# Load order at the start, and the row layout of w2, in an attention and MLP training step

## The chip, the cores and the metric

The kernel runs on one core of one Trainium2 chip. The metric is device time in microseconds, the median of several executions. Most executions of one kernel lie within 0.3% of each other. Ratios are the mean time of one kernel's runs over the mean of the other's runs of the same rounds, so they are not quite the ratio of the medians quoted beside them.

Engines: PE multiplies matrices (PEld is its weight load), DVE and ACT work element by element, POOL and SP here mostly issue DMA. SBUF is the core's on-chip memory of 128 partitions, PSUM the one that PE writes its sums to. The profile's line numbers (L451) are lines of the kernel; the change shifts them by one to ten.

## The reference

Forward and backward pass of a decode step: one token, 32 heads of attention over a cache of 8,192 positions, plus a gated MLP, in bf16. All gradients are outputs.

```python
xn = layernorm(x)                                  # D = 640
q = xn @ wq                                        # 32 heads of 128
p = softmax(q . k_cache * 128**-0.5)               # per head, 8192 positions
a = (p @ v_cache) @ wo
b = (silu(xn @ w1) * (xn @ w3)) @ w2               # F = 1728
out = x + a + b
# outputs: out and the gradients of x, k_cache, v_cache, wq, wo, w1, w3, w2
```

K, V and their gradients are 2 MB per head each. They make up 268 of the 304.6 MB that are moved. w1, w2 and w3 are 2.2 MB each.

## The kernel before

Ten SBUF slots of 2 MB hold K and V tiles. A head's K tile is overwritten by the gradient of K, stored, and its slot is loaded with a later tile; V likewise. Loads and large stores go through one queue, SP's, in program order. The MLP runs once, between heads 1 and 2, and borrows four slots (`mA` to `mD`). Its gradients go out through POOL's queue.

```python
load_group(0, nc.sync)              # wq and wo of heads 0 to 3: rows of 1,024 and 1,280 B
for _ in range(4):
    load_next()                     # K0, V0, K1, V1: 16,384 B per partition
mC = free_slots.pop(0); mD = free_slots.pop(0); ...
w2a = mD[:, 0:NBA * D].rearrange("p (b c) -> p b c", c=D)          # NBA = 12
fifo(w2a, B_w2[0:NBA * P, :].rearrange("(fb p) c -> p fb c", p=P)) # row fb*128+p: 1,280 B pieces
fifo(w1a, ...); ...                                                # then w1, w3, K2, V2

def store(kind, h):
    t = kv_tiles.pop((kind, h))
    ...
    fifo((dkc if kind == "K" else dvc)[h], t[:])   # gradient out
    free_slots.append(t)
    load_next()                     # next load; it waits until its slot's store has landed

def mlp():
    for wi in range(2):             # gate and up
        for b, rows in blocks_f:    # 13 blocks of 128 hidden units and one of 64
            for ci in range(NC):
                nc.tensor.matmul(gu_ps[0:rows, wi, b:b + 1],
                                 lhsT=wrow(wi, ci)[:, b * P:b * P + rows], rhs=xn_col_bf[:, ci:ci + 1], ...)
    ...                             # w2a * g, summed on PE; hcol, dgu from the sums
    for b in range(NBA):
        nc.vector.tensor_scalar(w2a[:, b, :], g_bc[:], hcol[:, b:b + 1], None, ALU.mult)
    nc.gpsimd.dma_start(out_8[0:NBA * P, :].rearrange("(fb p) c -> p fb c", p=P), w2a)
    ...
    for wi in range(2):
        for b0 in range(0, NB, 4):
            ...                     # PE turns dgu columns into rows, in PSUM tile pb
            nc.scalar.copy(bc_sb[:, wi, f0:f1], pb[:, 0:f1 - f0])
    ...                             # w1 and w3: products with bc_sb, gradients, stores by POOL
```

## Time and profile before

| | before |
|---|---|
| median of the first three runs, us | 749.35 (748.56 to 749.82) |
| profiled run, us | 747.4 |
| bytes moved, mean rate | 304.6 MB, 409 GB/s |
| steady rate, 160 to 300 us | 425 GB/s |

The page of the kernel before, cut: the engines' busy time, the DMA share and the rate in 40 equal slices of the span, and the chain of work that ended last.

```profile
PE 596.1 (80%) x11263; PEld 568.4 (76%) x11263; DVE 447.8 (60%) x739; ACT 333.4 (45%) x668; POOL 30.4 (4%) x45
...
DMA  8999999999999999999999999999999999999991
GB/s 327 387 413 421 426 425 425 395 427 426 416 426 427 428 421 428 425 428 425 424 424 429 426 425 417 415 417 424 420 413 425 418 417 419 419 415 418 408 402 72
...
DMA 48%; PE 39%; DVE 8%; issue 2%; ACT 1%; SPq 0%; ACTq 0%; DVEq 0%
```

No engine is full, but the DMA row reads 9 in 38 of 40 slices. So this kernel is bound by DMA, and the question for any change is whether it makes bytes move faster or keeps the DMA engines from running out of work. The rates name the weak places: the first two slices, the eighth (395), and the last (72).

The view by stretches resolves them. After the stretch and its length stand the busy times of PE, PEld, DVE, ACT and POOL; the last three numbers are granted PE clock, DMA share and GB/s.

```profile
2.00:4.00 2.00, 0.00 (x0) 0.00 (x0) 0.69 (x3) 1.09 (x1) 0.00 (x0) 1.00 0.57 139
4.00:6.00 2.00, 0.00 (x0) 0.00 (x0) 0.00 (x0) 0.00 (x0) 0.00 (x0) 1.00 0.77 201
...
28.00:34.00 6.00, 4.75 (x81) 4.29 (x80) 0.53 (x3) 5.07 (x11) 0.00 (x0) 1.00 1.05 333
...
130.00:135.00 5.00, 4.74 (x82) 4.68 (x83) 2.90 (x2) 3.36 (x7) 0.00 (x0) 1.00 0.97 382
135.00:140.00 5.00, 5.00 (x96) 4.86 (x94) 1.28 (x7) 4.15 (x10) 0.00 (x0) 1.00 1.00 367
```

At 28 to 34 us the share is full but the rate is 333: small packets. By the trace's packet records, w2's 1,280 B packets took a mean of 63.4 ns on each of 16 engines, which is 16 x 1,280 / 63.4 or 323 GB/s; K's and V's 16,384 B packets took 621 ns, 422 GB/s. At 130 to 140 us the packets are large, and yet the rate drops.

The timeline around that dip (start, length, engine, line, what):

```profile
116.55 0.33 SPq L101 DMA_DIRECT2D kv<-in_A_v_cache_dram  x1
116.93 0.81 SPq L101 DMA_DIRECT2D out_dram<-kv  x1
...
120.36 2.28 DVE L379 TENSOR_TENSOR kv<-qd,U 128x4096 bf16<-128x4096 bf16 x1
...
130.25 0.33 SPq L101 DMA_DIRECT2D kv<-in_A_k_cache_dram  x1
130.62 0.59 SPq L101 DMA_DIRECT2D out_dram<-kv  x1
```

DVE finishes the gradient of K of head 2 at 122.64 us, but its store is issued at 130.62. In between, SP holds a load that waits until the w3 gradient's store has left slot `mB`. The ready store stands behind it: SP's queue is in order.

How long the MLP's stores take is in the DMA view (queue, count, KB each, median us from issue to landing; the first line is w1's and w3's gradients, the second w2's):

```profile
out_dram<-kv POOLq DMA_DIRECT2D x2, 1728.0 KB, 37.0
out_dram<-kv POOLq DMA_DIRECT2D x1, 1920.0 KB, 24.2
```

The MLP itself, in the timeline: the gate and up products, the ACT copies of gradient rows, and the first DVE product that needs them.

```profile
55.82 1.21 PE L451 MATMUL gu_ps<-xn_col_bf,kv 128*128 128x1 bf16 x43
59.37 3.24 PE L451 MATMUL gu_ps<-xn_col_bf,kv 128*128 128x1 bf16 x97 [2.34 <-issue]
...
72.29 3.48 ACT L525 CAST kv<-pT 128x512 bf16<-128x512 f32 x8 [3.76 <-PE pT L520]
...
75.24 4.16 DVE L533 TENSOR_TENSOR KT<-kv,kv 128x1024 bf16<-128x1024 bf16 x7
```

### The profile page before, as it was taken

To read this page: it belongs to the slowest core of one execution; us is meant where nothing else is said; L and a number is where in the kernel's file an instruction comes from. 1 tells how busy PE (TensorE), PEld (TensorE's weight loads), DVE (VectorE), ACT (ScalarE), POOL (GpSimd) and SP (SyncE) were. 2 spreads that over 40 slices of the span, in tenths; PEclk is the share of its full clock that TensorE was granted. 3 is DMA by queue.
4 is the path that set the end of the run, shared out by engine and by line. 5 is a ranking of instruction groups with operands and counts; after the bars stand their busy time and mean duration, and the time that the engine had idled before them with its cause. 6 is when DMAs were issued, how large, how long until landed. Compare 5 with 4: busy or idle time off the path is not lost.

```text
span 745.6 us, 25013 instructions
## 1 busy us (share of the span) xinstructions
PE 596.1 (80%) x11263; PEld 568.4 (76%) x11263; DVE 447.8 (60%) x739; ACT 333.4 (45%) x668; POOL 30.4 (4%) x45
## 2 busy tenths in 40 slices
PE   1987698999999779888787897778798788979920
PEld 1886598988998778877686896778798787869820
DVE  4169937677767456656555763646556664656580
ACT  1641055555565355535355553445454353554500
POOL 0100200000000100001000000000000000000000
PEclk9997799999999889999999999998999899988965
DMA  8999999999999999999999999999999999999991
GB/s 327 387 413 421 426 425 425 395 427 426 416 426 427 428 421 428 425 428 425 424 424 429 426 425 417 415 417 424 420 413 425 418 417 419 419 415 418 408 402 72
DMA packets 29136, 304.63 MB, mean 409 GB/s; under 512 B 2836, under 2 KB 5972, under 8 KB 12644
## 3 DMA queue, kind: packets, MB, share of 16 engines
q1 hardware_dynamic: 22736, 276.39, 88.5%
q0 software_dynamic: 5984, 26.30, 8.8%
q8 instruction: 88, 1.44, 0.7%
q10 hardware_dynamic: 308, 0.33, 0.1%
q14 instruction: 20, 0.16, 0.1%
HBM read 151.67 MB, written 151.34 MB: 406 GB/s over the span
## 4 chain that ended last, share of the span: by engine, by line
DMA 48%; PE 39%; DVE 8%; issue 2%; ACT 1%; SPq 0%; ACTq 0%; DVEq 0%
DMA kv<-in_A_k_cache_dram 31%; PE pT L274 17%; DMA out_dram<-kv 13%; PE hb L358 6%; PE hb L373 4%; PE sA L293 4%; DMA kv<-in_A_v_cache_dram 4%; PE dA L293 4%; DVE kv L379 3%; DVE U L365 1%; PE sA L320 1%; PE dh_ps L462 1%; PE hb L363 1%; PE acc L536 1%; PE gu_ps L451 1%
## 5 line engine op out<-in xcount | busy, mean ns | idle before, releaser
L274 PE MATMUL pT<-ident_f,kv 128*128 128x128 f32 x2048 | 337.1, 289 | 67.4 <-DMA kv<-in_A_k_cache_dram 62.4
L276 ACT COPY KT<-pT 128x512 f32<-128x512 f32 x512 | 299.3, 586 | 182.6 <-PE pT L274 149.4
L274 PEld LDWEIGHTS pT<-ident_f,kv 128*128 128x128 f32 x2048 | 224.6, 145 | 71.5 <-issue 69.6
L293 PEld LDWEIGHTS <-KT 128*128 128x128 bf16 x4096 | 196.8, 100 | 17.7 <-issue 10.6
L379 DVE TENSOR_TENSOR kv<-qd,U 128x4096 bf16<-128x4096 bf16 x64 | 146.0, 2284 | 0.0
L379 DVE TENSOR_TENSOR kv<-qd,P 128x4096 bf16<-128x4096 bf16 x64 | 143.4, 2282 | 0.0
L293 PE MATMUL dA<-cz,KT 128*128 128x64 bf16 x2048 | 107.6, 197 | 8.0 <-ACT qd L310 5.8
L293 PE MATMUL sA<-cz,KT 128*128 128x64 bf16 x2048 | 102.7, 192 | 0.4 <-issue 0.3
L358 PEld LDWEIGHTS <-kv 128*128 128x128 bf16 x2048 | 81.7, 106 | 16.5 <-issue 16.5
L358 PE MATMUL hb<-P,kv 128*128 128x64 bf16 x2048 | 82.3, 202 | 14.3 <-DVE U L365 14.3
L375 ACT COPY od_g<-hb 128x2 f32<-128x2 f32 x32 | 5.1, 160 | 160.9 <-PE hb L373 160.9
L373 PE MATMUL hb<-U,kv 128*128 128x64 bf16 x2048 | 70.8, 194 | 5.1 <-issue 5.1
L373 PEld LDWEIGHTS <-kv 128*128 128x128 bf16 x2048 | 66.9, 98 | 6.0 <-issue 5.8
L349 DVE SCALAR_TENSOR_TENSOR U<-dA,P 128x64 bf16<-128x64 f32 x32 | 7.4, 232 | 93.7 <-PE dA L293 93.7
L316 DVE TENSOR_REDUCE mrow<-sA 128x1 f32<-128x64 f32 x32 | 7.2, 224 | 79.5 <-PE sA L293 79.5
L365 DVE SCALAR_TENSOR_TENSOR U<-dA,hb,P 128x128 bf16<-128x128 f32 x32 | 11.4, 355 | 36.3 <-PE hb L363 36.3
L429 DVE SCALAR_TENSOR_TENSOR wq_g<-wq_g,side 128x512 bf16<-128x512 bf16 x40 | 27.3, 683 | 0.0
L340 DVE RECIPROCAL rZ<-sA 128x1 f32<-128x1 f32 x32 | 5.4, 168 | 35.9 <-PE sA L334 35.0
L233 DVE SCALAR_TENSOR_TENSOR side<-wo_g,g_bc 128x640 bf16<-128x640 bf16 x32 | 26.2, 818 | 0.3
L323 DVE TENSOR_REDUCE negM<-sA 128x1 f32<-128x128 f32 x32 | 9.3, 291 | 18.6 <-PE sA L320 18.6
L424 POOL DMA_DIRECT2D out_dram<-wo_g x8 | 6.1, 761 | 295.5 <-DVE cz L298 262.3
L433 POOL DMA_DIRECT2D out_dram<-wq_g x8 | 6.9, 863 | 254.3 <-DVE wq_g L431 254.3
(134 smaller groups left out, 311.5 us busy)
## 6 DMA issues: line engine op xcount, KB each, us to landing
out_dram<-kv SPq DMA_DIRECT2D x64, 2048.0 KB, 31.8
kv<-in_A_k_cache_dram SPq DMA_DIRECT2D x32, 2048.0 KB, 26.9
kv<-in_A_v_cache_dram SPq DMA_DIRECT2D x32, 2048.0 KB, 26.9
out_dram<-wo_g POOLq DMA_DIRECT2D x8, 640.0 KB, 12.1
out_dram<-wq_g POOLq DMA_DIRECT2D x8, 640.0 KB, 13.3
wq_g<-in_A_wq_dram POOLq DMA_DIRECT2D x7, 640.0 KB, 13.8
wo_g<-in_A_wo_dram POOLq DMA_DIRECT2D x7, 640.0 KB, 19.5
kv<-in_B_w_dram SPq DMA_DIRECT2D x2, 1728.0 KB, 16.1
```

What stands on the lines that cost most here:

```text
L233: nc.vector.scalar_tensor_tensor(junk[:], G_["wo"][:, hh, :], 1.0, g_bc[:], ALU.mult, ALU.mult, accum_out=G_["do"][:, hh:hh + 1])
L274: nc.tensor.transpose(pT[:, k * P:(k + 1) * P], W3[:, 4 * c + k, :], ident_f[:])
L276: nc.scalar.copy(KT[:].rearrange("p k w -> p (k w)"), pT[:])
L293: nc.tensor.matmul(S_[kind][:, 0:J], lhsT=KTb[:, k, par, :], rhs=S_["cz"][:, o:o + J], start=(i == 0 and par == 0), stop=(par == 1), skip_ ...
L320: nc.tensor.matmul(S_["K"][:, J:J + P], lhsT=S_["mrow"][:].to_broadcast([P, P]), rhs=ident_f[:], start=False, stop=True, skip_group_check= ...
L323: nc.vector.tensor_reduce(S_["negM"][:], S_["K"][:, J:J + P], AX.X, ALU.max, negate=True)
L358: nc.tensor.matmul(S_["hb"][:, 0:RW], lhsT=V3[:, j, :], rhs=S_["P2"][:, j, 0:1].to_broadcast([P, RW]), start=(j == 0), stop=(j == J - 1), ...
L363: nc.tensor.matmul(S_["hb"][:, 2 * RW:2 * RW + 1], lhsT=negones_b, rhs=S_["rdot"][:], start=False, stop=True, skip_group_check=True)
L365: nc.vector.scalar_tensor_tensor(S_["U2"][:], S_["V"][:, 0:J].unsqueeze(2).to_broadcast([P, J, 2]), S_["hb"][:, 2 * RW:2 * RW + 1], S_["P2 ...
L373: nc.tensor.matmul(S_["hb"][:, RW:2 * RW], lhsT=K3[:, j, :], rhs=S_["U2"][:, j, 0:1].to_broadcast([P, RW]), start=False, stop=(j == J - 1) ...
L379: nc.vector.tensor_tensor(dst[:, lo * DH:hi * DH].rearrange("p (j a b) -> p j a b", a=DH // 2, b=2), vec.rearrange("p (a b) -> p a b", b=2 ...
L429: nc.vector.scalar_tensor_tensor(wq_g[:, ci, :], wq_g[:, ci, :], 1.0, dqb, ALU.mult, ALU.mult, accum_out=dxa[:, ci, g:g + 1])
```

## The change

The intent: start the transfer stream with large packets, and move w2 and its gradient in 15,360 B packets (twelve consecutive rows on each partition) in place of 1,280 B pieces. The second has a price. Hidden unit 12p + b now sits on partition p, block b, so the gate and up products must take w1's and w3's columns twelve apart, and the gradient rows must be scattered back into order.

```diff
+    load_next()
     load_group(0, nc.sync)
-    for _ in range(4):
+    for _ in range(3):
         load_next()
 ...
-    fifo(w2a, B_w2[0:NBA * P, :].rearrange("(fb p) c -> p fb c", p=P))
+    fifo(w2a, B_w2[0:NBA * P, :].rearrange("(p fb) c -> p fb c", fb=NBA))
 ...
+    def fcols(row, b, rows):
+        if b < NBA:
+            return row[:, 0:NBA * P].rearrange("p (f b) -> p b f", b=NBA)[:, b, :]
+        return row[:, b * P:b * P + rows]
 ...
-    ... lhsT=wrow(wi, ci)[:, b * P:b * P + rows],
+    ... lhsT=fcols(wrow(wi, ci), b, rows),
 ...
-        nc.gpsimd.dma_start(out_8[0:NBA * P, :].rearrange("(fb p) c -> p fb c", p=P), w2a)
+        nc.gpsimd.dma_start(out_8[0:NBA * P, :].rearrange("(p fb) c -> p fb c", fb=NBA), w2a)
 ...
+                if b0 < NBA:
+                    nc.scalar.copy(bc_sb[:, wi, 0:NBA * P].rearrange("p (f b) -> p b f", b=NBA)[:, b0:b0 + bn, :],
+                                   pb[:, 0:bn * P].rearrange("p (b f) -> p b f", f=P))
+                    continue
```

More of the change, by code (lines that the diff above doesn't have):

```diff
@@ L450, in mlp @@
                 for ci in range(NC):
-                    nc.tensor.matmul(gu_ps[0:rows, wi, b:b + 1], lhsT=wrow(wi, ci)[:, b * P:b * P + rows],
+                    nc.tensor.matmul(gu_ps[0:rows, wi, b:b + 1], lhsT=fcols(wrow(wi, ci), b, rows),
                                      rhs=xn_col_bf[:, ci:ci + 1], start=(ci == 0), stop=(ci == NC - 1))
```

## The prediction

> **What bounds the kernel now.** DMA. The page's DMA row reads 9 in all slices but the first and last; 304.6 MB move at a mean of 409 GB/s, and in steady stretches (the view by stretches) at 420 to 433 GB/s with a share of 1.0. PE is busy 80%, DVE 60%. In the DMA queue's waits, 544 us are loads waiting for a store to free a slot. So only DMA time counts. Four places lose some:
>
> 1. 2 to 6 us: share 0.57 to 0.77, 139 to 201 GB/s. The weight group goes first, in 1,024 and 1,280 B packets (mean 67 and 62 ns on 16 engines: 245 to 332 GB/s). K of head 0 lands at 15.1 us (chain of waits).
> 2. The w2 load, 28 to 34 us: 1,536 packets of 1,280 B, 282 to 364 GB/s.
> 3. The w2 gradient's store (issued 75.0 us, landed 24.2 us later), in 5,120 B packets: beside 16,384 B packets it got 205 of 840 KB per 2 us.
> 4. 130 to 140 us: 382 and 367 GB/s. K's gradient of head 2 was ready at 122.6 us, but its store was issued at 130.6, behind a load that waited for the w3 gradient's store.
>
> **What changes.**
> - K first: 16 KB packets start the stream, the small ones queue behind. I take most of the 1.3 us idle in 2 to 6 us: -1.0 us. Weights land at about 13.5 us instead of 9; the four DVE products on them (3.5 us) end near 17, when K's transposes are done, so head 0 starts as before or 1 us sooner.
> - w2 in 15,360 B packets: 1.97 MB at 332 GB/s is 5.9 us, at the 422 of the 16 KB packets 4.7: -1.3 us. The store, 404 to 422 GB/s: -0.2 us. The Trainium skill ("DMA: Bandwidth & Descriptors", Queues, rings and completion order) says each DMA engine alternates between queues packet by packet; the 205 to 640 KB in place 3 agrees (5,120/16,384). With near-equal packets the store should land in about 12 us, the other gradients' stores follow sooner, and the dip of place 4 shrinks: -1 us.
> - Strided weights: 120 of the 140 weight loads of the gate and up products read columns 24 B apart. The skill ("SBUF — State Buffer", note on cachelines) says bf16 strides beyond 8 elements pay a penalty; no run here shows it yet. They now run at about 30 ns a pair; at an estimated 55 to 110 ns that is 3 to 9 us, and it delays the MLP, since DVE and PE finish there together (62.6 us). Six ACT copies of 620 ns get a scattered output, maybe twice as slow: up to 1.5 us more.
> - But in 60 to 95 us the queues hold 15 us or more of issued work, so an MLP late by 3 to 6 us starves nothing at once, and head 2's stores now wait 4 to 8 us anyway. I charge +0.5 us.
>
> Sum: -3 us. Predicted 746.0 us, 8 times in 10 between 742.0 and 750.0. Faster by over 2%: 0.01; within: 0.97; slower: 0.02.
>
> **In the profile after:** 2 to 6 us near 400 GB/s; w2's load over 400 GB/s; its store landing in 10 to 16 us; 130 to 140 us over 400 GB/s; gate/up weight loads slower and the MLP several us longer, with DMA share still 1.0.
>
> **What would make it wrong:** an MLP over 8 us late, leaving the queues empty before head 2's stores; small packets costing as much behind K as before; w2's store taking turns from loads that heads 2 to 4 wait for.

## The result, and the profile after

| | before | after |
|---|---|---|
| median of 6 runs, us | 749.0 (747.93 to 749.82) | 746.48 (746.32 to 747.02) |
| ratio | 1 | 0.9969, interval 0.9956 to 0.9982 |
| profiled run, us | 747.4 | 746.44 |

The gain is 0.3%: clear of the noise, and inside the class "same" at 2%. The page after, cut to the rates and the chain:

```profile
GB/s 338 402 414 422 425 428 427 426 424 425 425 424 424 426 421 427 426 429 424 424 421 420 425 419 410 418 416 423 423 410 424 411 424 400 421 416 417 407 402 74
...
DMA 49%; PE 36%; DVE 8%; ACT 2%; issue 1%; SPq 0%; ACTq 0%; DVEq 0%
```

In the first half three slices differ by more than 10: the first two (338 and 402 in place of 327 and 387) and the eighth (426 in place of 395). The same stretches as above:

```profile
2.00:4.00 2.00, 0.00 (x0) 0.00 (x0) 0.69 (x3) 0.95 (x1) 0.00 (x0) 1.00 0.65 218
4.00:6.00 2.00, 0.00 (x0) 0.00 (x0) 0.00 (x0) 0.00 (x0) 0.00 (x0) 1.00 0.93 361
...
28.00:34.00 6.00, 4.75 (x89) 4.30 (x86) 0.77 (x5) 5.09 (x10) 0.00 (x0) 1.00 0.96 371
...
130.00:135.00 5.00, 4.50 (x133) 4.30 (x131) 3.57 (x5) 0.62 (x2) 0.00 (x0) 1.00 1.03 431
135.00:140.00 5.00, 4.61 (x81) 4.55 (x82) 3.62 (x2) 3.23 (x7) 0.00 (x0) 1.00 0.99 423
```

The stores of the MLP's gradients take ten to twelve microseconds less from issue to landing. On the clock they land 4 to 8 us sooner, as all are issued later (w2's at 91.75 us in place of 99.21, w3's at 126.17 in place of 130.23):

```profile
out_dram<-kv POOLq DMA_DIRECT2D x2, 1728.0 KB, 24.9
out_dram<-kv POOLq DMA_DIRECT2D x1, 1920.0 KB, 14.6
```

And the blocked store is gone. In the timeline, SP's load of the freed slot goes at 126.19 us, while DVE is still at work on the gradient of K of head 2, and the store follows DVE's end (128.37) at once. Two things moved here: the load goes 4.1 us sooner, and the gradient is ready 5.7 us later than before, because the MLP is late. So the store itself is issued only 2.2 us sooner; the list under e8 shows why that is enough.

```profile
126.09 2.28 DVE L380 TENSOR_TENSOR kv<-qd,U 128x4096 bf16<-128x4096 bf16 x1
...
126.19 0.33 SPq L101 DMA_DIRECT2D kv<-in_A_k_cache_dram  x1
128.40 0.34 SPq L101 DMA_DIRECT2D out_dram<-kv  x1
```

The MLP, on the other hand, is 6.1 us later:

```profile
55.47 2.68 PE L457 MATMUL gu_ps<-xn_col_bf,kv 128*128 128x1 bf16 x43
58.59 5.68 PE L457 MATMUL gu_ps<-xn_col_bf,kv 128*128 128x1 bf16 x97 [0.45 <-issue]
...
74.38 6.92 ACT L530 CAST kv<-pT 128x512 bf16<-128x512 f32 x3 [3.90 <-PE pT L526]
...
81.33 4.17 DVE L543 TENSOR_TENSOR KT<-kv,kv 128x1024 bf16<-128x1024 bf16 x7 [3.92 <-ACT kv L530]
```

By the chain of waits, the first 43 strided pairs of weight load and product took 2.52 us, 59 ns each, where they had taken 1.05 us, 24 ns each. The three scattered copies took 2.31 us each, where all eight of before, six of them this large, took 3.48 us. DVE waits 3.92 us for them. So the change makes 6 us of engine work in the MLP appear, and still the kernel is faster.

### A ruler for small differences

Differences of 1 us drown in a total of 749. A better ruler is the time at which the first N MB have been moved, taken from the packet records of each trace: bytes summed in order of the packets' starts, instruction packets left out, times from the start of the span and interpolated between packets. The kernel before reaches 10, 20, 52, 60, 150 and 302 MB at 28.02, 53.68, 129.71, 149.88, 362.72 and 727.99 us. This table gives the difference to it, in us (negative is sooner):

| run | 10 MB | 20 MB | 52 MB | 60 MB | 150 MB | 302 MB |
|---|---|---|---|---|---|---|
| before again (e7) | -0.11 | -0.24 | -0.39 | -0.42 | -0.38 | +0.50 |
| the change | -0.56 | -1.14 | -1.69 | -2.83 | -2.71 | -0.94 |
| the change again (e0) | -0.59 | -1.21 | -1.43 | -2.19 | -2.03 | -0.26 |
| e1, K first | -0.58 | -0.54 | -0.68 | +1.33 | +1.52 | +1.12 |
| e2, w2 layout | -0.25 | -1.03 | -1.39 | -2.63 | -2.56 | -1.05 |
| e3, w2 load only | -0.16 | -0.78 | -0.69 | -1.75 | -1.70 | -0.60 |
| e4, w2 store only | -0.06 | -0.09 | -0.37 | -1.53 | -1.53 | -0.40 |
| e5, MLP late | -0.11 | -0.23 | -0.55 | -1.19 | -0.80 | +0.31 |
| e6, copy order | -0.56 | -1.17 | -1.45 | -2.79 | -2.50 | -1.17 |
| e8, K first, store order | -0.52 | -0.49 | -0.77 | -1.95 | -1.72 | -0.52 |

The first 10 MB hold the start, 10 to 20 MB the w2 load, 52 to 60 MB the dip. The two profiles of the same kernel before agree within 0.42 us up to 150 MB and part by 0.9 us after that, so only the columns up to 150 MB are used as a ruler.

### The profile page after: what moved, and what is told of

The parts are those of the page before. It is cut to its first block, busy times and chain, and to the rows that moved or that the text cites. A ratio compares the mean times of both kernels' runs of the same rounds, so it can differ in the third digit from the quotient of the medians.

```text
span 744.7 us, 25012 instructions
## 1 busy us (share of the span) xinstructions
PE 598.0 (80%) x11263; PEld 570.5 (77%) x11263; DVE 448.0 (60%) x739; ACT 344.0 (46%) x668; POOL 29.9 (4%) x45
## 4 chain that ended last, share of the span: by engine, by line
DMA 49%; PE 36%; DVE 8%; ACT 2%; issue 1%; SPq 0%; ACTq 0%; DVEq 0%
DMA out_dram<-kv 25%; PE pT L275 15%; DMA kv<-in_A_k_cache_dram 15%; DMA kv<-in_A_v_cache_dram 8%; PE hb L359 5%; PE sA L294 4%; PE hb L374 4%; DVE kv L380 4%; PE dA L294 3%; DMA wo_g<-in_A_wo_dram 2%; PE gu_ps L457 1%; ACT kv L530 1%; DVE U L366 1%; PE dh_ps L468 1%; PE sA L321 1%
## 5 line engine op out<-in xcount | busy, mean ns | idle before, releaser
L366 DVE SCALAR_TENSOR_TENSOR U<-dA,hb,P 128x128 bf16<-128x128 f32 x32 | 11.4, 355 | 36.2 <-PE hb L364 36.2
L311 ACT CAST qd<-dA 128x256 bf16<-128x256 f32 x31 | 11.5, 373 | 12.4 <-DVE kv L380 9.5
## 6 DMA issues: line engine op xcount, KB each, us to landing
out_dram<-wq_g POOLq DMA_DIRECT2D x8, 640.0 KB, 13.5
```

The source lines that it names most:

```text
L311: nc.scalar.copy(qd[:].rearrange("p a d -> p (a d)"), hd[h].pop("ps_r"))
L366: nc.vector.scalar_tensor_tensor(S_["U2"][:], S_["V"][:, 0:J].unsqueeze(2).to_broadcast([P, J, 2]), S_["hb"][:, 2 * RW:2 * RW + 1], S_["P2 ...
```

## The experiments

All but two gave right results; e3 and e4 are wrong on purpose. "Before" is the median of the before kernel in the same rounds.

| run | before, us | this, us | ratio (interval) |
|---|---|---|---|
| e1 K first | 748.71 | 748.51 | 0.9997 (0.9984 to 1.0009) |
| e2 w2 layout | 748.71 | 746.71 | 0.9976 (0.9963 to 0.9988) |
| e3 w2 load only | 748.71 | 747.09 | 0.9982 (0.9970 to 0.9995) |
| e4 w2 store only | 748.71 | 746.80 | 0.9977 (0.9963 to 0.9990) |
| e5 MLP late | 748.55 | 748.97 | 1.0002 (0.9989 to 1.0014) |
| e6 copy order | 748.55 | 746.26 | 0.9973 (0.9959 to 0.9986) |
| e0 the change again | 748.55 | 747.30 | 0.9978 (0.9966 to 0.9991) |
| e7 before again | 748.82 | 749.05 | 1.0002 (0.9989 to 1.0015) |
| e8 K first, store order | 748.82 | 747.47 | 0.9986 (0.9974 to 0.9999) |
| e10 copy and store order | 748.82 | 746.41 | 0.9968 (0.9954 to 0.9981) |
| e11 w1, w3 rows | 748.43 | 747.32 | 0.9983 (0.9969 to 0.9997) |

My theory after the result: only DMA time counts; the gain is the sum of the start, the w2 load, and a dip that went because a ready store is no longer stuck behind a waiting load; the late MLP costs nothing. The rivals are named in each expectation.

### e1: K first alone

```diff
+    load_next()
     load_group(0, nc.sync)
-    for _ in range(4):
+    for _ in range(3):
```

> Before with K of head 0 first, nothing else. Theory (the start is worth about half a microsecond, read from the two traces: the first 10 MB were moved 0.56 us sooner): 0.3 to 1.0 us less than before; 10 MB moved about 0.5 us sooner; dip at 130 to 140 us still there (about 375 GB/s). Rival (the order at the start is worth 1 us or more, and the whole 2.5 us could come from it): 1.5 us less or better.

The start gains what was expected: 10 MB 0.58 us sooner. The total does not: 0.2 us by the medians, a ratio of 0.9997, short of the 0.3 us that was expected. The stretches and SP's issues show where it went:

```profile
130.00:135.00 5.00, 5.00 (x84) 4.84 (x83) 1.78 (x2) 4.18 (x8) 0.00 (x0) 1.00 0.74 263
135.00:140.00 5.00, 5.00 (x101) 4.95 (x98) 3.13 (x7) 3.90 (x9) 0.00 (x0) 1.00 0.99 321
```

```profile
132.29 0.33 SPq L101 DMA_DIRECT2D kv<-in_A_k_cache_dram  x1
132.67 0.83 SPq L101 DMA_DIRECT2D out_dram<-kv  x1
```

The dip got deeper: 263 and 321 GB/s, a share of 0.74, and head 2's K store is issued at 132.67 us, 2 us later than before. Between 52 and 60 MB this kernel loses 2.0 us. By the ruler more than was won at the start is given back there: at 60 MB this kernel is 1.33 us behind. The total does not show that excess.

### e2: the w2 layout alone

```diff
     (the whole change, except:)
-    load_next()
     load_group(0, nc.sync)
-    for _ in range(3):
+    for _ in range(4):
```

> The change without K first: both w2 transfers in 15,360 B packets, with the strided weight loads and the scattered ACT copies. Theory (load 0.7 us, stores and the dip at 130 to 140 us 1.4 us): 1.5 to 2.2 us less than before, no dip. Rival (layout gives back in the late MLP what it wins in transfers): within 0.5 us of before.

2.0 us less, as the theory had it, and no dip (424 GB/s over 130 to 140 us). Nearly all of the change's gain is in the layout. The rival, that the late MLP gives the layout's gain back, falls.

### e3: only the w2 load (wrong results)

```diff
-    fifo(w2a, B_w2[0:NBA * P, :].rearrange("(fb p) c -> p fb c", p=P))
+    fifo(w2a, B_w2[0:NBA * P, :].rearrange("(p fb) c -> p fb c", fb=NBA))
```

> Before with only the w2 load in 15,360 B packets; no stride anywhere, results wrong on purpose (rows of w2 meet the wrong hidden units). Theory: 12 MB are moved 0.7 to 1.2 us sooner, and the dip at 130 to 140 us stays, as the store still has 5,120 B packets: 0.5 to 1.2 us less in all. Rival (the load alone makes the whole gain): 2 us less.

Partly missed. Between 10 and 20 MB it gains 0.62 us, as expected for the load. But the dip is gone too, though the store still has 5,120 B packets and still takes 24.2 us:

```profile
130.00:135.00 5.00, 5.00 (x91) 4.92 (x88) 2.60 (x2) 3.74 (x8) 0.00 (x0) 1.00 1.02 423
135.00:140.00 5.00, 5.00 (x94) 4.87 (x92) 1.76 (x7) 4.15 (x9) 0.00 (x0) 1.00 1.01 426
```

In this run the load that blocks SP was issued at 127.81 us in place of 130.25. By the packet records, SP's queue moved only 57 GB/s at 116 to 118 us and nothing at 118 to 120 (188 and nothing in the kernel before), so POOL's stores had the engines to themselves for longer and were done sooner. That 2.4 us is enough to close the dip, although the ready store (DVE ends at 122.36) still waits 5.8 us, to 128.19. The dip is thus an edge: a shift of about 2 us of one store, either way, opens it (e1) or closes it (e3). Why the shift went this way with this edit is read from one profile and is an argument, not a test.

### e4: only the w2 gradient's store (wrong results)

```diff
-        nc.gpsimd.dma_start(out_8[0:NBA * P, :].rearrange("(fb p) c -> p fb c", p=P), w2a)
+        nc.gpsimd.dma_start(out_8[0:NBA * P, :].rearrange("(p fb) c -> p fb c", fb=NBA), w2a)
```

> Before with only the w2 gradient's store in 15,360 B packets; no stride, MLP as early as before, results wrong on purpose (rows of the gradient in other places). Theory (larger packets win larger turns, the stores behind them land sooner, so no load holds up head 2's K store): store lands in 10 to 15 us instead of 24, the w1 and w3 stores land 8 to 10 us sooner, no dip at 130 to 140 us, 1.0 to 1.6 us less. Rival (the dip went because the MLP is 6 us late, not because of packets): dip stays near 375 GB/s and the time is within 0.5 us of before.

As the theory said, except that its 1.9 us by the medians lies a little over the range, and that w1's and w3's stores land 7.7 us sooner after their issue (29.3 in place of 37.0), not 8 to 10:

```profile
out_dram<-kv POOLq DMA_DIRECT2D x2, 1728.0 KB, 29.3
out_dram<-kv POOLq DMA_DIRECT2D x1, 1920.0 KB, 14.8
```

```profile
130.00:135.00 5.00, 5.00 (x84) 4.84 (x83) 1.51 (x2) 4.18 (x8) 0.00 (x0) 1.00 1.00 423
135.00:140.00 5.00, 5.00 (x101) 4.96 (x98) 3.13 (x7) 3.90 (x9) 0.00 (x0) 1.00 1.01 428
```

The MLP is as early here as before, so its lateness is not needed for the dip to go. Of the 1.53 us at 60 MB, 1.16 us come between 52 and 60 MB.

The gains of e3 (1.6 us) and e4 (1.9 us) do not add up to that of e2 (2.0 us), because each alone closes the same dip, and it can be closed once.

### e5: the MLP late, all packets as before

```diff
-                nc.scalar.copy(bc_sb[:, wi, f0:f1], pb[:, 0:f1 - f0])
+                for _ in range(5):
+                    nc.scalar.copy(bc_sb[:, wi, f0:f1], pb[:, 0:f1 - f0])
```

> Before with every ACT copy of the MLP's gradient rows made five times over (same values): the MLP ends about 6 us later, all packets as before. Theory (an MLP late by 6 us starves nothing, and does not remove the dip either): within 0.7 us of before, GB/s at 130 to 140 us or some us after still low. Rival 1 (lateness removes the dip): 1 us or more less than before, no dip. Rival 2 (lateness costs time): 1.5 to 6 us more.

The first w1 store is issued at 90.0 us in place of 82.2, the last w3 store at 100.2 in place of 92.3. The time is 748.97 us against 748.55, a ratio of 1.0002. So an MLP 8 us late costs nothing that can be measured. The rates say that lateness also softens the dip:

```profile
130.00:135.00 5.00, 4.20 (x100) 3.85 (x97) 2.39 (x7) 2.09 (x4) 0.00 (x0) 1.00 1.00 393
135.00:140.00 5.00, 4.53 (x106) 4.38 (x103) 5.00 (x3) 1.72 (x4) 0.00 (x0) 1.00 1.01 401
```

393 and 401 in place of 382 and 367, and 0.64 us between 52 and 60 MB: about half of the dip. This did not reach the total, and rival 1, that lateness alone makes the gain, falls. But the store is no longer blocked in this run. Its gradient is ready at 130.21 us, in place of 122.64, and it goes at once, about as late as before:

```profile
129.34 0.33 SPq L101 DMA_DIRECT2D kv<-in_A_k_cache_dram  x1
130.23 0.34 SPq L101 DMA_DIRECT2D out_dram<-kv  x1
```

So lateness removes the block and puts itself in its place. That it is free fits the 8 us that the store had waited for its turn anyway.

### e0: the change again

Unedited, for comparison with e5 and e6 on the same chip.

> The change itself on this chip, for comparison with the runs beside it: 2.0 to 3.0 us less than before, 382 and 367 GB/s of before at 130 to 140 us replaced by over 415.

Missed by some tenths: 1.25 us less by the medians, 1.65 by the ratio. The first set of runs gave 2.5 us by the medians and 2.3 by the ratio (1 - 0.9969, of 749). The intervals overlap; the honest size of the gain is about 2 us. The stretch 130 to 140 us moved at 414 GB/s here, just under the 415 that were expected, and the gain between 52 and 60 MB is 0.76 us in place of 1.14. Head 2's K store is issued at 129.71 us, when its late gradient is ready.

### e6: the same values, copied in another order

```diff
-  nc.scalar.copy(bc_sb[:, wi, 0:NBA * P].rearrange("p (f b) -> p b f", b=NBA)[:, b0:b0 + bn, :],
-                 pb[:, 0:bn * P].rearrange("p (b f) -> p b f", f=P))
+  nc.scalar.copy(bc_sb[:, wi, 0:NBA * P].rearrange("p (f b) -> p f b", b=NBA)[:, :, b0:b0 + bn],
+                 pb[:, 0:bn * P].rearrange("p (b f) -> p f b", f=P))
```

> The change with the six scattered ACT copies walking the output in runs of four neighbouring bf16 (8 B) instead of single ones 24 B apart; same values. If the stride of the write made them slow (2.32 us against 0.60): 0.6 to 1.2 us each, MLP 3 to 5 us shorter. If not: still 2.3 us or more, as the read of PSUM now jumps 512 B. Theory on time (MLP lateness is free): within 0.7 us of the change in either case. Rival (lateness costs): 1 to 2 us less than the change if the copies get faster.

The copies fall from 2.31 to 0.52 us each (three in 1.56; one instruction alone lasts 0.62 us in the median, as expected), and DVE no longer waits for them:

```profile
74.46 1.56 ACT L530 CAST kv<-pT 128x512 bf16<-128x512 f32 x3 [3.70 <-PE pT L526]
...
77.41 4.16 DVE L543 TENSOR_TENSOR KT<-kv,kv 128x1024 bf16<-128x1024 bf16 x7
```

Compared with the change, the w1 products start 3.9 us sooner (77.41 us in place of 81.33). The total is 746.26 us, where the change had 746.48 in its first rounds and 747.30 beside this run; by the ratios 0.9973 and 0.9978, whose intervals overlap widely. Up to 60 MB its ruler agrees with the change's within 0.25 us. So 3.9 us saved on ACT and DVE are worth nothing clear of the noise. The comparison with the change's first rounds (746.48) agrees with the theory; the one beside it differs by 1.04 us in medians, over the 0.7 of the theory and inside the rival's 1 to 2 us, but by the ratio only 0.4 us.

### e9: runs of two bf16

```diff
+  for j in range(0, bn, 2):
-  ... [:, :, b0:b0 + bn], pb[:, 0:bn * P] ...
+  ... [:, :, b0 + j:b0 + j + 2], pb[:, j * P:(j + 2) * P] ...
```

> As the version with the reordered copy, but each copy writes runs of two bf16 (4 B) 24 B apart, 256 elements each, 12 copies. If the cost sits on writes of a single bf16 (4.5 ns each in the change's copies): 0.3 to 0.45 us a copy. If it sits on every separate run: 128 runs of 4.5 ns, 0.7 us a copy or more. Time as the version with the reordered copy.

The group view of that line (least, median and greatest ns of one instruction):

```profile
L531 ACT CAST kv<-pT x12: 391/474/551, 74.9 to 78.0; 128x256 bf16<-128x256 f32 x12
```

The median is 0.47 us, just over the range of the first reading; the timeline has six of them in 1.80 us, 0.30 each. The cost is thus not one per separate run. It sits on single bf16 values written 24 B apart: 4.5 ns per element there, 1.0 with runs of four, 1.2 with runs of two. The one run was 746.55 us, its state unknown.

### e7: before again

> The kernel before, unchanged, for a second profile of it and as a control of the timing. Its ratio should be 1.000 within 0.0013. If the late part of the first profile of before (its run was 747.4 us against a median of 749.0) was a lucky one, this profile moves the same 302 MB 1 us or more later, with the same dip at 130 to 140 us.

749.05 against 748.82 us, ratio 1.0002. The profile has the same dip (409 and 360 GB/s) and moves 302 MB 0.5 us later than the first one, and 0.9 us later when counted from 150 MB. So a part of what looks like a loss of the change after 150 MB in the table belongs to a lucky first profile; the expected 1 us or more was too much.

### e8: K first, and head 2's store ahead of the waiting load

This is the direct test of the blocked store: the kernel with the deepest dip, with one load moved behind one store.

```diff
 def store(kind, h):
     ...
     free_slots.append(t)
-    load_next()
+    if (kind, h) != ("V", 2):
+        load_next()
+    if (kind, h) == ("K", 2):
+        load_next()
```

> K first alone (748.5 us) with one more edit: the load issued behind head 2's V store is moved behind its K store, so that the K store no longer stands behind a load that waits for the w3 gradient's store. All packets of w2 as before. Theory (the dip is that blocked store, which empties the queue): K store of head 2 issued by about 124 us instead of 132.7, 130 to 140 us at over 400 GB/s instead of 292, 1.5 to 2.5 us less than before. Rival (the slow 1.0 to 1.9 us packets of that stretch have another cause, for example the mix of loads and stores): dip stays, time within 0.7 us of before.

SP's issues, and the stretches:

```profile
123.23 0.34 SPq L101 DMA_DIRECT2D out_dram<-kv  x1
129.90 0.34 SPq L101 DMA_DIRECT2D kv<-in_A_k_cache_dram  x1
```

```profile
130.00:135.00 5.00, 4.12 (x71) 4.07 (x72) 3.44 (x2) 2.86 (x6) 0.00 (x0) 1.00 1.02 432
135.00:140.00 5.00, 5.00 (x83) 4.85 (x82) 0.69 (x5) 4.03 (x10) 0.00 (x0) 1.00 1.00 423
```

The store goes at 123.23 us, 9.4 us sooner than in e1, and the dip is closed, from 263 and 321 to 432 and 423 GB/s, with not one packet changed. At 60 MB e8 is 3.3 us ahead of e1. The rival (mixed traffic as such) falls: in the kernel with K first, the blocked store is the cause of the dip.

The other profiles sharpen this. What goes with the dip is how late the store is issued, whether it was blocked or its data were late:

| K store of head 2 issued, us | waited after its data, us | GB/s, 130 to 140 us |
|---|---|---|
| 132.67 (e1) | 11.4 | 292 |
| 130.62 (before), 130.08 (e7) | 8.0, 8.2 | 374, 385 |
| 130.23 (e5) | 0.0 | 397 |
| 129.71 (e0) | 0.0 | 414 |
| 128.40 (the change), 128.19 (e3), 127.90 (e2) | 0.0, 5.8, 0.0 | 427, 424, 424 |
| 126.72 (e6), 124.73 (e10), 123.68 (e4), 123.23 (e8) | 3.6, 0.0, 2.6, 0.0 | 426, 422, 425, 427 |

How a late store lowers the rate is seen only in part. In the kernel before, 14.4 packets are in flight on average at 130 to 132 us, where steady stretches have 16.1: some engines have no work. But at 136 to 138 us the share is 1.05, and 16,384 B packets take 862 ns on average in place of 621. Both are gone in e8 (16.1 in flight, 615 ns). Why the packets slow down is not shown.

In total the time is 747.47 us, 1.35 us less than before by the medians and 1.0 by the ratio; e1 had 0.2. That is right in sign and less than the 1.5 to 2.5 us that were expected. The intervals of e8 and e1 overlap, so the gain of the reorder over e1 is shown by the rates and the ruler, and not by the total.

### e10: copy order and store order on the change

```diff
     (the edit of e6 and the edit of e8, on the change)
```

> The change with the reordered copy and head 2's K store ahead of the load. The change has no dip left, so theory says the store order adds nothing: 745.5 to 746.8 us, no more than 0.7 us from the version with the reordered copy alone (746.3). Rival (there is still time lost behind blocked stores): 1 us or more less.

746.41 us, ratio 0.9968; e6 had 0.9973. As expected: where the dip is gone, the store order has nothing left to win.

### e11: w1 and w3 in consecutive rows as well

The experiments pointed to a layout whose permutation costs no engine time: five consecutive rows of the input dimension per partition for w1, w3 and wq. Then only the five columns of x that are made at the start are permuted.

```diff
-    w1_v = B_w1.rearrange("(ci p) f -> p ci f", p=P)
+    w1_v = B_w1.rearrange("(p ci) f -> p ci f", ci=NC)      # likewise w3, wq and the three gradients
 ...
+    (x and grad_out columns made in the same order; the gradient of x stored from [128, 5], 10 B each)
```

> The version with the reordered copy, and w1, w3, wq and their gradients with five consecutive rows of the input dimension per partition, so that w1 and w3 move in 13,824 B packets instead of 3,456 (loads) and 6,912 (stores). The permutation falls on the five columns of x that are made once at the start, so no strided weight load in the MLP and no scattered copy comes with it. Theory (only DMA time counts): 3.9 MB at 400 GB/s become 421: 20 MB moved 0.4 to 0.6 us sooner than with the reordered copy alone, w1 and w3 stores land sooner, 0.3 to 0.8 us less in all, about 745.7 us; hardly clear of the noise, so the moved bytes decide. Rival (3,456 B is large enough, nothing to win): 20 MB at the same time within 0.15 us.

Missed. Its ratio to before is 0.9983, e6's 0.9973; it beats nothing. Between 12 and 16 MB, where w1 and w3 are loaded, it gains 0.5 us on e6 by the packet records, as intended, but the first 12 MB come 0.27 us later than in e6, and at 20 MB it is 0.15 us behind. At 302 MB the two are equal (0.05 us apart). The end costs more: the last DMA is issued at 727.68 us and the span ends at 745.5, 17.8 us later; in e6 it is issued at 728.36 and the span ends at 744.4, 16.0 us later. The gradient of x goes out there in 128 packets of 10 B in place of 5 of 256 B. They are not what lands last: in both runs that is the gradient store issued at 716.8 to 716.9 us, which lands at 744.37 in e11 and 743.28 in e6. The 10 B packets run until 738.5 us. That they hold the last store up is possible, but no run separates it. No version here beats the change clear of the noise.

## Why the prediction was right

The prediction was 746.0 us in a range of 742.0 to 750.0; measured were 746.48. It was right in total and in its mechanism. The range was wide enough to hold the kernel before itself (749.0), so that lying inside it says little; the terms say more. One by one:

- **"K first: ... -1.0 us."** The mechanism held, the size was twice too large. The engines' idle time at 2 to 6 us did not all go: 218 and 361 GB/s, not "near 400", and 8 to 10 us runs at 303. Small packets did not cost as much behind K as before: those of 1,024 B took 52 ns in place of 67. (The 62 ns of the prediction mixes wo's packets, 56 ns, with w2's, 63.4.) 10 MB are moved 0.5 us sooner (e1: 0.58, before again: 0.11). Alone it is worth nothing in total, because the dip deepens (e1). The landing of the weights was put at 13.5 us; the first DVE product that needs wo starts at 14.38, and the four end at 17.9 in place of 17. Head 0's PE work ends 0.36 us sooner (38.37 in place of 38.73 us).
- **"w2 in 15,360 B packets: ... -1.3 us."** About half: 0.6 us between 10 and 20 MB (the change 0.58, e3 0.62, e2 0.78, before again 0.13). The term took 422 GB/s for w2's new packets; their mean was 639 ns, so 16 x 15,360 / 639 or 384 GB/s. And "over 400 GB/s" for that stretch was 371. The "-0.2 us" for the store does not show: e4, which has it alone, is 0.37 us ahead at 52 MB, and the control e7 is 0.39.
- **"The dip ... -1 us."** Right, and the largest term: 1.1 to 1.2 us between 52 and 60 MB in the change, e2, e4 and e8 (0.76 in the change again). The store landed in 14.6 us ("about 12", "10 to 16"). The Trainium skill's statement on turns (DMA: Bandwidth & Descriptors, Queues, rings and completion order) carried this term, and the trace agrees again: with packets of 15,360 beside 16,384 B, the w2 store got 1,920 KB and SP's queue 2,256 KB at 80 to 90 us, 0.85 to 1, where before it had been 205 to 640.
- **"at an estimated 55 to 110 ns that is 3 to 9 us."** 59 ns was inside, at the low end; the gate and up stage grew from 6.6 to 8.6 us, by 2.0, because a gap of 2.34 us in it shrank to 0.45. The cacheline note of the skill (SBUF — State Buffer, Door 1) agrees in both places here: single bf16 24 B apart are slow to read (59 against 24 ns a pair) and to write (4.5 ns each), while two or four neighbours per 24 B (e9, e6) cost about 1.0 to 1.2 ns each.
- **"Six ACT copies ... maybe twice as slow: up to 1.5 us more."** Mis-sized: about four times as slow (2.31 us, against at most 3.48 / 6 or 0.58), and DVE waited 3.92 us. So the MLP is 6.1 us late as foretold ("3 to 6 us"), but mostly through the copies and not through the weight loads; that the two errors cancel is luck.
- **"I charge +0.5 us" for the late MLP.** Rather 0: e5 is 8 us late and measures 1.0002; e6 takes 3.9 us out again and gains nothing clear. The reason given held too ("head 2's stores now wait 4 to 8 us anyway"): the K store waited 8.0 us before, and in the change its gradient is 5.7 us later and it waits for nothing.

The sum of measured pieces is 0.5 + 0.6 + 1.2, or 2.3 us, the same as the ratio says (2.3 us of 749), against -3 in the prediction. Three terms were too large, by 0.5, 0.7 and 0.2 us; against them stand a dip weighed 0.2 us too small and a charge of 0.5 us that was not due. That the errors partly cancel is luck. So, in part, is the agreement of the pieces with the total, for what the ruler shows need not reach the end: e8 is 3.3 us ahead of e1 at 60 MB and 1.0 us in total, the 0.64 us of e5 gained nothing, and the change again gave 1.65 us.

What stays open: in the profiles, the change's lead of 2.7 us at 150 MB is 0.9 at 302 MB (1.4 when compared with the second profile of before). Other early winners lose some of their lead too, and e1, which is behind, catches up 0.4. The two profiles of the kernel before differ by 0.9 us in the same stretch, so a real give-back of some tenths cannot be told from the spread of single profiles. The six timed runs show 2.3 us at the end.

One more thing is open, and it is larger than the gain. The view by stretches of the kernel before shows the end of the span:

```profile
735.00:740.00 5.00, 0.00 (x0) 0.00 (x0) 0.00 (x0) 0.00 (x0) 0.00 (x0) 0.50 0.06 26
740.00:745.60 5.60, 0.00 (x0) 0.00 (x0) 0.00 (x0) 0.00 (x0) 0.00 (x0) 0.50 0.04 18
```

By the packet records, from about 731 us to 744 only one packet is in flight at a time, where steady stretches have 16; in the change it is so from about 730 to 743 us. So far as these records tell, the end is set by what one of the 16 DMA engines still has queued, and not by the mean rate. This can be why gains on the ruler do not reach the total one for one. Which engine lags, and why, is not in the record; no version here touches these 13 us.

## What to carry to other kernels

When the DMA row is full, cost a change in bytes moved per microsecond and in whether a queue runs dry, and let work off that path be slower as long as its results come in time: here 6 us more were free, because the store that needed them had waited 8 us for its turn. Look at the last slice as well: here a single packet at a time for 13 us sets the end. In an in-order issue queue, look for a ready store behind a load that waits for someone else's store; it can be found in the timeline by comparing when the data were ready with when the store was issued, and a small reorder closes it without any new layout (e8). Gains that close the same gap do not add, and a gain ahead of such a gap may be lost in it, so test the parts of a change one by one and together.

## What the Trainium skill lacked or had wrong

- DMA: Bandwidth & Descriptors (Specifications) gives 512 B as the smallest transfer for line rate. Here 1,024 B packets moved at 245 GB/s in the kernel before (mean 67 ns) and at 317 in the change, behind K (52 ns), and 1,280 B packets of w2 at 323 (63.4 ns), against 422 for 16,384 B packets (621 ns). Perfetto Trace Analysis (DMA Optimizations) says that small DMAs, under 2 KB, have significant overhead per transfer; if that is read of each packet, these runs agree with it.
- The same page (Where 436 GB/s comes from) says that the HBM side, about 358 GB/s per core, binds transfers between HBM and SBUF, though its own measured table reaches 425 for 16 MB, and a note beside the table keeps about 358 for the case that both cores of an HBM domain stream. The sentence lacks that condition: with one core at work, this kernel held 425 GB/s from 160 to 300 us.
- TensorE: Matmul & The Clock Gate (Weight-path perf modes) allows strided weights for the fast load and gives no cost for the stride. A column step of 12 bf16 took 59 ns per pair of weight load and one-column product, against 24 ns without it.
- ScalarE: Activation LUTs has no figure for a scattered output. 512 single bf16 24 B apart took 2.31 us, the same values in runs of four 0.52 us (e6), in contiguous order at most 0.58 us.
- No page that I read warns of a ready store held up in an in-order issuing queue by a load that waits for another queue's store: 8 us of waiting in the kernel before, and 1.2 us on the ruler between 52 and 60 MB.
